# A GpSimd memset moved behind the first v load, with an early idle matmul waiting on it

## The chip, the cores and the metric

The kernel runs on one core of one Trainium2 chip. The metric is the device time of one execution in microseconds (us). The six executions of the kernel before that were timed beside the change lie from 288.93 to 289.5 us (0.2%). Ratios compare the mean time of one kernel's fast runs with the mean of the other's fast runs of the same rounds, on the same chip, so a ratio is not quite the ratio of the medians that stand beside it.

## The reference

Chunked attention (8 batches, 8 heads, 576 positions in chunks of 64, head size 64), followed by a two-layer network with a swish whose slope is learned:

```python
scores = scale * q_c @ k_c.T          # per chunk of 64
attn = softmax(scores)
x = (attn @ v_c)                      # rearranged to (4608, 512)
h = x @ w_in                          # (4608, 2048)
g = h * sigmoid(beta * h)
out = g @ w_out                       # (4608, 512), float32
```

## The kernel before

The network's matmuls fill the span: those of its two layers (L322 and L354 on the page) are busy for 136.7 and 131.3 us of 287.5. What matters here is the start, where the first attention blocks are made while the array's clock is still slow: the idle matmuls start mostly 0.427 us apart up to 7.23 us and 0.216 us apart from 9.00 us on (the trace's record of the clock has it fast from 7.69). TensorE's stream begins with 78 tiny matmuls and 14 idle ones on zeros, put there for the clock's sake, of which the fourth (16 columns wide) reads `late`, so that it waits on a memset by GpSimd. `emit_T_half(0)` uses the raw first half of q and k, cast by ScalarE; `emit_T_half(1)` uses the second half ("the q half", "the k half" below), loaded and cast by GpSimd's own transfers.

```python
nc.vector.memset(tiny, 0.0)
nc.vector.memset(idle, 0.0)
nc.vector.memset(braw, 0.0)
nc.vector.memset(vbig[:, :, :, D:D + 1], 1.0)
for a, eng, dst in ((0, nc.sync, raw0), (1, nc.gpsimd, qk0[1])):
    for i, src in enumerate((q, k)):
        eng.dma_start(out=dst[i], in_=...)      # the second pair: q half, k half
...                                             # beta, by the sync queue
nc.gpsimd.memset(late, 0.0)
for i in range(4):
    load_v(i)
...                                             # identity, weights, further loads
emit_tiny(78)
warm = idle_bank()
emit_idle(3, 512, warm)
nc.tensor.matmul(out=warm[:, 0:16], lhsT=idle[:, 0:128], rhs=late)
emit_idle(10, 512, warm)
emit_T_half(0)                                  # VectorE transposes q and k, first half
emit_sc_half(0, 0)                              # first scores
emit_ex_half(0, 0)
emit_idle(6, 512, idle_bank())                  # (shortened)
emit_T_half(1)                                  # second half: needs q half and k half
nc.vector.transpose(out=bt, in_=braw)
emit_sc_half(0, 1)                              # second scores
emit_ex_half(0, 1)
emit_sc_half(1, 0)
emit_idle(2, 512, warm)
emit_pv(0, ("s", "p"))                          # needs v loads 0 and 1
...
```

The softmax here doesn't subtract the row's maximum and nothing guards it: scores larger than these inputs give would overflow.

## Time and profile before

| | kernel before |
|---|---|
| time, median of 3 (range) | 288.98 us (288.93 to 289.1) |
| span in the profile | 287.5 us |
| TensorE busy | 281.2 us, 98% |
| k half, from issue to landing | 2.12 to 9.74 us |
| second scores start | 10.91 us |

The prediction shows the lines of the page, the chain and the timeline. A chain is read from the bottom up: each piece was released by the one above it. A timeline line gives start, length, engine, source line, operation and count; a bracket at its end gives the idle time of the engine just before and what ended it.

### The profile page before, as it was taken

The page shows a single profiled execution, that of the slowest core. Times are in us where ns is not written, and L with a number is a line of the kernel's source. Part 1 is how long each engine was busy: PE and PEld are TensorE (multiplying, and loading weights), DVE is VectorE, ACT ScalarE, POOL GpSimd, SP SyncE. Part 2 cuts the span into 40 slices and gives each one's busy share as a digit, 9 for nine tenths or more (in the row PEclk, how much of TensorE's full clock was granted, in tenths as well). Part 3 has the DMA queues.
Part 4 walks back from the last instruction along what each step waited for, and adds up shares of the span by engine and source line. Part 5 has one row for each costly group of instructions (what it writes and reads, how often), then busy time and mean ns, then how long its engine had stood idle before and what let it go on. Part 6 is the DMA issues. An engine that isn't in the chain of part 4 may idle for free.

```text
span 287.5 us, 6650 instructions
## 1 busy us (share of the span) xinstructions
PE 281.2 (98%) x2779; PEld 136.2 (47%) x2779; DVE 141.4 (49%) x253; ACT 146.7 (51%) x224; POOL 95.7 (33%) x125
## 2 busy tenths in 40 slices
PE   8889999999999999999999999999999999999995
PEld 4464456545544444444444444444444444444444
DVE  2678444776567554534454445444453536333300
ACT  4377218774557545454545454555445544444411
POOL 8743579397172992060907060000000000000000
PEclk9999999999999999999999999999999999999999
DMA  8999999999999999999999999614252212010012
GB/s 197 174 197 206 169 178 209 211 163 173 153 94 182 155 176 179 153 130 159 132 167 134 145 155 142 134 49 110 75 113 73 73 39 73 36 39 36 36 73 75
DMA packets 139997, 37.14 MB, mean 129 GB/s; under 512 B 126912, under 2 KB 135488, under 8 KB 139968
## 3 DMA queue, kind: packets, MB, share of 16 engines
q0 software_dynamic: 99136, 17.83, 79.7%
q1 hardware_dynamic: 40688, 18.83, 30.5%
q8 instruction: 22, 0.36, 0.5%
q14 instruction: 7, 0.06, 0.1%
q10 hardware_dynamic: 144, 0.07, 0.1%
HBM read 36.71 MB, written 9.44 MB: 161 GB/s over the span
## 4 chain that ended last, share of the span: by engine, by line
PE 94%; DMA 3%; ACT 1%; issue 1%; DVE 0%; POOL 0%; DVEq 0%; POOLq 0%
PE hps L322 44%; PE ops L354 42%; DMA h<-in_k_dram 3%; PE x L264 2%; PE sc L236 1%; PE sc L223 1%; PE ops L580 1%; ACT xt L297 1%; PE xp L296 1%; PE sc L196 0%; ACT et L206 0%; POOL h L394 0%; PE warm L374 0%; PE xp L304 0%; DVE xt L297 0%
## 5 line engine op out<-in xcount | busy, mean ns | idle before, releaser
L336 DVE SCALAR_TENSOR_TENSOR gt<-sg,hps 128x512 f16<-128x512 f32 (+1 forms) x153 | 99.1, 654 | 108.5 <-ACT sg L332 108.3
L332 ACT ACTIVATE sg<-hps,beta 128x512 f32<-128x512 f32 (+1 forms) x153 | 100.4, 663 | 74.0 <-PE hps L322 73.9
L322 PE MATMUL hps<-xt,win 128*128 128x512 f16 (+1 forms) x612 | 136.7, 367 | 0.8 <-ACT xt L297 0.7
L354 PE MATMUL ops<-wout,gt 128*128 128x512 f16 x560 | 131.3, 379 | 0.0
L322 PEld LDWEIGHTS <-win 128*128 128x128 f16 x612 | 58.0, 98 | 61.9 <-issue 1.0
L354 PEld LDWEIGHTS <-gt 128*128 128x128 f16 x560 | 53.7, 98 | 63.1
L364 ACT ACTIVATE osb<-ops 128x512 f32<-128x512 f32 x35 | 20.9, 598 | 42.2 <-PE ops L354 42.2
L112 POOL DMA_DIRECT2D vbig<-in_v_dram x40 | 34.0, 872 | 10.3 <-DMA wout<-in_moe_w_out_dram 3.7
L98 POOL DMA_DIRECT2D qu<-in_q_dram x22 | 18.7, 865 | 39.5 <-DMA qT<-qu 37.2
L280 DVE TENSOR_TENSOR x<-x,rd 128x512 f16<-128x512 f32 x34 | 23.5, 692 | 1.3
L98 POOL DMA_DIRECT2D ku<-in_k_dram x22 | 18.9, 880 | 0.1
L278 DVE RECIPROCAL rd<-x 128x8 f32<-128x8 f32 x34 | 6.8, 201 | 11.1 <-PE x L264 11.1
L245 ACT ACTIVATE et<-sc 128x1024 f16<-128x1024 f32 (+1 forms) x8 | 6.4, 811 | 8.2 <-PE sc L236 8.2
L229 ACT ACTIVATE et<-sc 128x1024 f16<-128x1024 f32 x10 | 10.1, 1015 | 0.0
L264 PEld LDWEIGHTS <-et 64*64 64x64 f16 x576 | 6.0, 107 | 7.3 <-issue 3.4
L374 PE MATMUL warm<-idle 128*128 128x512 f16 x24 | 8.6, 515 | 0.0
L264 PE MATMUL x<-vbig,et 64*64 64x65 f16 x544 | 7.8, 195 | 0.2 <-ACT et L206 0.2
L104 POOL DMA_DIRECT2D ku<-in_k_dram x9 | 6.8, 755 | 2.5 <-DMA win<-in_moe_w_in_dram 1.3
L104 POOL DMA_DIRECT2D qu<-in_q_dram x9 | 6.8, 767 | 1.9 <-DMA win<-in_moe_w_in_dram 1.1
L592 DVE TENSOR_SCALAR osb<-ops 128x256 f32<-128x256 f32 (+1 forms) x2 | 0.7, 358 | 12.1 <-PE ops L580 12.1
L130 POOL DMA_DIRECT2D win<-in_moe_w_in_dram x8 | 6.0, 751 | 1.2 <-DMA h<-in_k_dram 0.8
L177 DVE STREAM_TRANSPOSE t<-h 128x512 f32<-128x512 f32 x4 | 4.2, 1084 | 4.2 <-ACT h L176 3.7
(46 smaller groups left out, 69.3 us busy)
## 6 DMA issues: line engine op xcount, KB each, us to landing
out_dram<-osb SPq DMA_DIRECT2D x35, 256.0 KB, 3.4
vbig<-in_v_dram POOLq DMA_DIRECT2D x32, 128.0 KB, 7.6
qu<-in_q_dram POOLq DMA_DIRECT2D x20, 128.0 KB, 5.3
ku<-in_k_dram POOLq DMA_DIRECT2D x20, 128.0 KB, 6.6
win<-in_moe_w_in_dram POOLq DMA_DIRECT2D x8, 256.0 KB, 9.7
wout<-in_moe_w_out_dram POOLq DMA_DIRECT2D x4, 512.0 KB, 12.4
qu<-in_q_dram POOLq DMA_DIRECT2D x3, 256.0 KB, 7.3
ku<-in_k_dram POOLq DMA_DIRECT2D x3, 256.0 KB, 8.9
```

Of the source, the lines that this page charges most:

```text
L98: nc.gpsimd.dma_start(out=tv[off:off + n, sp], in_=src[b, :, s:s + n, :].rearrange("h p d -> p h d"),)
L104: nc.gpsimd.dma_start(out=t[off // 2:(off + n) // 2], in_=src[b, :, s:s + n, :].rearrange("h (p r) d -> p h r d", r=2),)
L112: nc.gpsimd.dma_start(out=vbig[off:off + n, i, :, 0:D], in_=v[b, :, s:s + n, :].rearrange("h p d -> p h d"),)
L229: nc.scalar.activation(out=et, in_=sc, func=ACTF.Exp, scale=scale)
L264: nc.tensor.matmul(out=(x[0][64 * c:64 * c + 64, r, g, 0:D + 1] if len(x) == 1 else x[r][64 * c:64 * c + 64, g, 0:D + 1]), lhsT=(et[64 * r ...
L280: nc.vector.tensor_tensor(out=o, in0=z[..., 0:D], in1=rd[:, r].to_broadcast(list(o.shape)), op=ALU.mult)
L322: nc.tensor.matmul(out=hps[:, 0:n], lhsT=w_in16[m // 2][:, kk, (m % 2) * 128:(m % 2) * 128 + 128], rhs=xr[:, c0 // CH:(c0 + n) // CH, 2 * ...
L332: nc.scalar.activation(out=sg[:, 0:n], in_=hps[:, 0:n], func=ACTF.Tanh, scale=beta2[:, m:m + 1])
L336: nc.vector.scalar_tensor_tensor(out=gt_t[j][:, m, c0:c0 + n], in0=sg[:, 0:n], scalar=1.0, in1=hps[:, 0:n], op0=ALU.add, op1=ALU.mult,)
L354: nc.tensor.matmul(out=ops, lhsT=gt_t[j][:, kk, t * 128:(t + 1) * 128], rhs=w_out16[kk // 4][:, kk % 4, :], start=(kk == 0), stop=(kk == K ...
L364: nc.scalar.activation(out=osb, in_=ops, func=ACTF.Copy, scale=0.5)
L374: nc.tensor.matmul(out=d[:, 0:w], lhsT=idle[:, 0:128], rhs=idle[:, 0:w])
```

## The change

The intent is to move the idle matmuls a little later by letting the matmul on `late` wait longer: the memset is issued behind the first v load instead of ahead of it.

```diff
-        nc.gpsimd.memset(late, 0.0)
         for i in range(4):
             load_v(i)
+            if i == 0:
+                nc.gpsimd.memset(late, 0.0)
```

## The prediction

> **What bounds the kernel now.** I read the page's busy shares first, then the chain of work that ended last, then the timeline of the first 18 us, and last the individual idle matmuls. From the page:
>
> ```profile
> span 287.5 us, 6650 instructions
> PE 281.2 (98%) x2779; PEld 136.2 (47%) x2779; DVE 141.4 (49%) x253; ACT 146.7 (51%) x224; POOL 95.7 (33%) x125
> PE hps L322 44%; PE ops L354 42%; DMA h<-in_k_dram 3%; PE x L264 2%; PE sc L236 1%; PE sc L223 1%; PE ops L580 1%; ACT xt L297 1%; PE xp L296 1%; PE sc L196 0%; ACT et L206 0%; POOL h L394 0%; PE warm L374 0%; PE xp L304 0%; DVE xt L297 0%
> ```
>
> The second line says that TensorE is busy nearly throughout; the third, that the chain is TensorE for 94% of the span, with one transfer of a k tile in it (3%). From 18.0 us on, the stage windows give 262.85 us busy of 263.00. Nothing in the change reaches that part except by the time at which it starts and the clock at which it starts. So the question is what the change does to the first 18 us. The chain over these 20 us, in order of time, begins:
>
> ```profile
> 1.24 0.88 POOL h L394
> 2.12 7.62 DMA h<-in_k_dram
> ...
> 9.77 0.06 DVE t L177
> ...
> 10.71 0.18 DVE bt L425
> ...
> 10.91 0.71 PE sc L196 x58
> ```
>
> Its columns are start, length and what. The path is: GpSimd issues the half of k that it casts on the way (from 2.12 us), this takes 7.62 us to land, VectorE transposes it from 9.77 us and then the beta tile from 10.71, and only at 10.91 does TensorE come onto the path. The idle matmuls before it are on no path[...]. The memset and its matmul lie here:
>
> ```profile
> 2.12 0.76 POOL L394 DMA_DIRECT2D h<-in_k_dram  x1
> 2.86 0.15 POOL L401 MEMSET late<- 128x16 f16 x1
> 2.90 3.54 POOL L112 DMA_DIRECT2D vbig<-in_v_dram  x4
> 2.12 1.46 PE L374 MATMUL warm<-idle 128*128 128x512 f16 x3
> 3.37 0.22 PE L417 MATMUL warm<-late,idle 128*128 128x16 f16 x1
> 3.44 4.41 PE L374 MATMUL warm<-idle 128*128 128x512 f16 x10
> 8.40 0.45 PE L196 MATMUL sc<-t,t 32*64 32x64 f16 x32 [0.55 <-DVE t L177]
> 8.78 1.47 PE L374 MATMUL warm<-idle 128*128 128x512 f16 x6
> 10.91 0.71 PE L196 MATMUL sc<-t,t 32*64 32x64 f16 x64 [0.66 <-DVE bt L425]
> ```
>
> (First the GpSimd timeline, then TensorE's: start, length, engine, line, what; the bracket is idle time ahead of it and its releaser.) The memset ends at 2.86 + 0.15 = 3.01 us. Its matmul starts at 3.37 with no bracket: it waits for nothing, since the three idle matmuls ahead occupy the array till then. **The wait is empty today**, by 0.36 us. Then the array is idle twice before the path reaches it: 0.55 us before 8.40 and 0.66 us before 10.91, both times for VectorE.
>
> [...] in the records of single instructions the idle matmuls start 0.427 us apart up to the last of the ten, at 7.231, and those after the first scores 0.216 us apart (9.000, 9.216, 9.432). So the fast clock came somewhere from 7.66 (7.231 + 0.427) to 8.40 or soon after. The column of granted clock reads 1.0 throughout; it doesn't show this. [...] four v loads take 3.54 us of GpSimd, 0.885 us each, one after another, and a memset behind one has to wait for it.
>
> **The change part by part.** No instruction is removed or added; one memset moves behind one v issue.
>
> *GpSimd.* The first v issue moves from 2.90 to about 2.86, 0.04 us earlier. It takes 0.885 us of its turn, so the memset runs at 2.86 + 0.885 = 3.74 and ends at 3.89. In the kernel before it overlapped its neighbours so far that it cost only 2.90 - 2.86 = 0.04 us, so the other three v loads start when they do now (3.78 for the second), and so does everything behind them. The k half on the path is issued at 2.12, ahead of all of this. Sum on the transfers: 0.00 on the path, 0.04 us earlier for one v load that is used at 12.08 and lands after about 7.6 us, near 10.5.
>
> *TensorE.* A finished memset released the first tiny matmul 0.05 us later (0.82 + 0.09 = 0.91, start at 0.96). So the matmul on `late` starts at 3.89 + 0.05 = 3.94 instead of 3.37: the wait becomes real, about 0.57 us of idle array. From this matmul to the last of the ten idle ones is 7.231 - 3.364 = 3.867 us, so the last starts at 3.94 + 3.87 = 7.81, and its 0.427 us of streaming end at 8.24. The scores can't start before 8.40, when VectorE releases them. **The 0.57 us come out of the idle stretch before 8.40** (7.66 to 8.40 is 0.74 us of real slack by start-to-start spacing), and 0.16 us of it are left. Sum on the scores: 0.00.
>
> *After that.* Even if the scores slipped by 0.1 or 0.2 us, the six idle matmuls end near 10.08 (9.863 + 0.216) and TensorE then waits until 10.91. That is 0.8 us of further cushion, and ScalarE's first exponential at 8.91 is followed by idle time until 11.41. So the direct sum on the path is 0.0 us.
>
> *Clock.* The new hole lies at 3.37 to 3.94. [...]
>
> **The rivals.**
>
> [...] Cost: six idle matmuls at 0.427 for 0.216 add 6 x 0.211 = 1.27 us, of which 0.8 us is cushion, so 0.45 us; the second scores and the two idle matmuls behind them at half speed (0.6 + 0.43 us now) add perhaps another 0.5 us: about +1 us, 290.0. Against it: three timed runs before lie within 0.17 us of each other[...]; and the new dense stretch runs from 3.94 almost without a hole to 10.1, longer than the old one from 2.11 to 7.66. In the extreme, [...] the 6 us or so of TensorE work from 10.9 to 18.0 (6.16 us busy) would nearly double: +6 us, 295. I hold this for very unlikely.
>
> *The hole makes the clock come earlier or the start better.* A reason to put a wait there would be to push idle work closer to the first scores[...]. But the clock is fast at 8.78 already, and no idle matmul before 10.91 is on the path, so there is nothing to win in this phase: 288.9 at best, unless timed executions of the kernel before often started cold beyond 10.9, which their narrow spread speaks against.
>
> *GpSimd is delayed.* If the memset between two software-made transfers costs its 0.15 us in full, or more for a change of task, all later issues shift by 0.1 to 0.3 us. The weights are needed at 15.62 and the ones on the path were issued before; k doesn't move. Cost 0 to 0.1 us, 289.1.
>
> **Range and chances.** Direct sum 0.0 us, so the middle is the time before, 289.0. The spread of executions (0.17 us here; the profiled run took 289.26) gives about 0.3 us either way; the later clock, at maybe one in seven, stretches the upper side by 1 us; hence 288.6 to 289.8. Two per cent is 5.8 us, more than anything in the first 18 us could give back, and only the extreme clock case reaches it upwards: faster 0.01, slower 0.02.
>
> **What would show it right or wrong.** In the changed profile: memset at about 3.74; matmul on `late` near 3.94, with idle time ahead of it put down to GpSimd; ten idle matmuls 0.427 us apart, the last at about 7.8; first scores still at 8.40 with the idle time ahead nearly gone; six idle matmuls behind them 0.216 us apart; k half landing near 9.75, second scores at 10.91, steady part from 18.0. Wrong if: the six idle matmuls are 0.427 apart (later clock); the first scores start when the idle matmuls let them, above 8.5; the k half lands at another time by over 0.2 us; or the memset finishes long after 3.9.

The prediction's sum came to 0.0 us (0.00 on the transfers, 0.00 on the scores), so to 289.0 us. Its range of 288.6 to 289.8 adds 0.3 us either way for the spread of executions and 1 us on the upper side for a later clock. The transfers called "software-made" are those of queue 0, which the page lists as `software_dynamic` (99136 packets).

## More of the kernel before

The view of the DMA queues, taken for 7.1 to 7.3 us of the kernel before, lists beside the data queues (columns: queue, kind, packets, megabytes, share of the time of the 16 engines):

```profile
q8 instruction: 1, 0.02, 29.2%
```

This is a packet of instructions: 16 KB, begun at 7.17 us and 0.93 us long by its record in the trace. The whole execution has 22 of them. From the first to the last, TensorE starts 5389 instructions (185 and 5574 started), which makes 257 between one and the next on average; singly it is 94 to 434. I take these packets to feed TensorE's instruction stream and call the first of them the fetch.

## The result

The changed kernel takes 289.55 us (median of 6, 289.34 to 289.81) against 289.13 (288.93 to 289.5) before: ratio 1.0014, 95% interval 1.0001 to 1.0027. By the 2% rule that is the same time; it is inside the predicted range, but 0.4 us above the kernel before, where the prediction's sum was 0.0.

The page of the changed kernel has the same shape:

```profile
span 287.7 us, 6650 instructions
PE 280.8 (98%) x2779; PEld 136.1 (47%) x2779; DVE 141.3 (49%) x253; ACT 146.7 (51%) x224; POOL 95.6 (33%) x125
```

The timeline of the start shows what was expected of GpSimd and TensorE:

```profile
2.86 0.91 POOL L112 DMA_DIRECT2D vbig<-in_v_dram  x1
3.73 0.16 POOL L404 MEMSET late<- 128x16 f16 x1
3.94 0.17 PE L418 MATMUL warm<-late,idle 128*128 128x16 f16 x1 [0.36 <-POOL late L404]
3.97 3.77 PE L374 MATMUL warm<-idle 128*128 128x512 f16 x10
8.42 0.45 PE L196 MATMUL sc<-t,t 32*64 32x64 f16 x32 [0.69 <-DVE t L177]
8.80 1.47 PE L374 MATMUL warm<-idle 128*128 128x512 f16 x6
11.21 0.71 PE L196 MATMUL sc<-t,t 32*64 32x64 f16 x64 [0.94 <-DVE bt L426]
```

The memset runs at 3.73 and its matmul at 3.94, so the hole is there. The first scores hardly move (8.42 for 8.40), and the six idle matmuls take 1.47 us as before, so the clock was fast in time. Yet the second scores start at 11.21 instead of 10.91. The chain says why:

```profile
2.13 7.93 DMA h<-in_k_dram
...
10.07 0.06 DVE t L177
...
11.01 0.18 DVE bt L426
...
11.21 0.71 PE sc L196 x62
```

The k half lands 0.31 us later (7.93 us for 7.62 from issue), and everything behind it is later by 0.30. I compared the start of every hundredth matmul of the two traces: from the 200th to the last, the changed kernel is 0.30 to 0.31 us behind at each one. So in these two profiles the loss is made before 11.2 us and carried to the end.

Why should a transfer issued at the same 2.12 us land later? The DMA view of the changed kernel for 7.9 to 8.1 us has the instruction packet that stood at 7.17 before:

```profile
q8 instruction: 1, 0.02, 30.4%
```

By its record it runs from 7.93 to 8.90 us. The landings tell the rest. The trace has 16 reports of the k half's landing, each of which I take for one share of the transfer (no record says what a report stands for): in the changed kernel 15 came by 8.68 us, and the last alone at 10.05. Before, 14 came by 8.67, one at 9.44 and the last at 9.74. In the changed kernel one share of the transfer is late by itself. And it stays behind: of each of the four v loads that follow, too, the last report comes 1.05 to 1.13 us after the fifteenth. The instruction packet of 16 KB took 0.97 us here, where one of 512 bytes in GpSimd's queue takes 0.06 us. If it holds up one share of the transfer, and not the others, it would do this. The packet records don't name a DMA engine, so this was a theory to be tested:

- **Theory A.** The wait on `late` holds up TensorE's instruction fetch. The later memset moves the fetch later by 0.76 us, onto the tail of the k half, which lands later.
- **Theory B.** The first v load, now issued 0.04 us earlier, takes DMA time from the k half.
- **Theory C.** The landing varies by itself, and the 0.4 us are noise.
- **The hole.** The idle time in the array itself costs, by way of the clock or otherwise.

### The profile page after: what moved, and what is told of

It is laid out like the page before. It is cut to its first block, busy times and chain, and to the rows that moved or that the text cites. A ratio compares the mean times of both kernels' runs of the same rounds, so it can differ in the third digit from the quotient of the medians.

```text
span 287.7 us, 6650 instructions
## 1 busy us (share of the span) xinstructions
PE 280.8 (98%) x2779; PEld 136.1 (47%) x2779; DVE 141.3 (49%) x253; ACT 146.7 (51%) x224; POOL 95.6 (33%) x125
## 3 DMA queue, kind: packets, MB, share of 16 engines
q0 software_dynamic: 99136, 17.83, 79.8%
HBM read 36.71 MB, written 9.44 MB: 160 GB/s over the span
## 4 chain that ended last, share of the span: by engine, by line
PE 93%; DMA 3%; ACT 1%; issue 1%; DVE 0%; POOL 0%; DVEq 0%; POOLq 0%
PE hps L322 44%; PE ops L354 42%; DMA h<-in_k_dram 3%; PE x L264 2%; PE sc L236 1%; PE sc L223 1%; PE ops L581 1%; ACT xt L297 1%; PE xp L296 1%; PE sc L196 0%; ACT et L206 0%; POOL h L394 0%; PE warm L374 0%; PE xp L304 0%; DVE xt L297 0%
## 5 line engine op out<-in xcount | busy, mean ns | idle before, releaser
L112 POOL DMA_DIRECT2D vbig<-in_v_dram x40 | 34.3, 881 | 10.1 <-DMA wout<-in_moe_w_out_dram 3.7
L229 ACT ACTIVATE et<-sc 128x1024 f16<-128x1024 f32 x10 | 10.1, 1015 | 0.0
```

The lines of the kernel that those rows point to most:

```text
L112: nc.gpsimd.dma_start(out=vbig[off:off + n, i, :, 0:D], in_=v[b, :, s:s + n, :].rearrange("h p d -> p h d"),)
L229: nc.scalar.activation(out=et, in_=sc, func=ACTF.Exp, scale=scale)
```

## The experiments

Times of the fetch, of the 16th report of the k half and of the memset are from the records in each run's trace; the second scores from its timeline. All runs gave correct results. Times from records can differ by 0.01 us from those of the views.

| run | memset ends | fetch starts | k half landed | second scores | median us | ratio to before (95%) |
|---|---|---|---|---|---|---|
| before | 3.00 | 7.17 | 9.74 | 10.91 | 289.13 | |
| change | 3.89 | 7.93 | 10.05 | 11.21 | 289.55 | 1.0014 (1.0001 to 1.0027) |
| aa_before | 3.00 | 7.18 | 9.75 | 10.91 | 289.09 | 0.9998 (0.9986 to 1.0010) |
| after_again | 3.89 | 7.99 | 10.06 | 11.23 | 289.55 | 1.0017 (1.0004 to 1.0030) |
| gap_only | 3.94 | 7.94 | 10.05 | 11.21 | 289.63 | 1.0013 (1.0001 to 1.0025) |
| v_early_only | 1.19 | 5.44 | 9.57 | 10.74 | 289.25 | 1.0013 (0.9997 to 1.0029) |
| tiny68 | 3.01 | 12.74 | 9.06 | 11.52 | 294.80 | 1.0190 (1.0159 to 1.0220) |
| after_tiny68 | 3.89 | 12.86 | 8.97 | 10.56 | 295.53 | 1.0199 (1.0166 to 1.0233) |
| late_after_v1 | 4.76 | 8.72 | 9.35 | 11.50 | 289.30 | 1.0000 (0.9982 to 1.0019) |
| tiny88 | 3.01 | 5.32 | 9.54 | 10.71 | 289.10 | 0.9994 (0.9979 to 1.0010) |
| after_tiny88 | 3.89 | 5.50 | 9.77 | 10.93 | 289.24 | 1.0002 (0.9985 to 1.0019) |
| late6_v1 | 4.77 | 8.91 | 8.71 | 10.18 | 288.63 | 0.9976 (0.9962 to 0.9991) |
| late8_v2 | 5.64 | 10.19 | 9.18 | 10.55 | 289.58 | 1.0015 (0.9996 to 1.0035) |
| late6_v0 | 3.89 | 7.80 | 9.88 | 11.05 | 289.48 | 1.0026 (1.0005 to 1.0047) |

### The two kernels again: aa_before, after_again

No edit.

> The kernel before, unchanged, timed against itself. All theories: ratio 1.000. It shows how far a ratio of the size measured for the change (1.0014) can come from noise alone: if this one departs from 1 by 0.001 or more, the 0.4 us of the change are not shown to be its own. In its profile the k half should land near 9.74 us, as in the first profile; if it lands anywhere from 9.4 to 10.1, the landing varies by itself.

> The changed kernel once more. Theory A (TensorE's later progress moves its instruction fetch, [...] from 7.17 to 7.93 us, onto the tail of the k half, which then lands at 10.05 instead of 9.74): fetch again near 7.9, k half near 10.05, ratio 1.001 to 1.002. Theory B (the first v load, issued 0.04 us earlier, takes DMA time from the k half): the same landing, with no tie to the fetch. Theory C (noise): ratio within 0.0005 of 1, the k half anywhere from 9.4 to 10.1.

Both held to theory A. The kernel before against itself gives 0.9998, with fetch and landing within 0.01 us of the first profile; the changed kernel again gives 1.0017, with fetch at 7.99 and landing at 10.06. Theory C falls: the landing does not vary by itself from 9.4 to 10.1; in the two profiles of each kernel it agrees within 0.01 us. The cost of the change is small but its own. One thing was not the same in after_again: a share of the raw k half landed at 6.92 us (6.18 in the first profile), so that VectorE released the first scores only at 9.15. The second scores started at 11.23 all the same, behind the k half.

The clock, by contrast, does vary. In the timeline of the kernel before, run again, the ten idle matmuls took 3.00 us instead of 4.41:

```profile
3.45 3.00 PE L374 MATMUL warm<-idle 128*128 128x512 f16 x10
8.37 0.45 PE L196 MATMUL sc<-t,t 32*64 32x64 f16 x32 [1.92 <-DVE t L177]
```

The trace's record of the clock has it fast from 4.86 us here and from 7.69 in the first profile of the same kernel, and the second scores start at 10.91 in both. So the moment of the fast clock does differ between executions, by 2.83 us in these two. In these two it cost nothing.

### One part of the change at a time: gap_only, v_early_only

```diff
# gap_only                                 # v_early_only
 nc.gpsimd.memset(late, 0.0)               -nc.gpsimd.memset(late, 0.0)
 for i in range(4):                        +nc.vector.memset(late, 0.0)   # ahead of braw's
     load_v(i)
+    if i == 0:
+        nc.gpsimd.memset(late, 0.0)
```

> The memset is done twice, at its old place and behind the first v issue; the matmul waits for the second. So the hole in TensorE is as in the changed kernel, but the first v load is issued at 2.90 us as in the kernel before. Theory A: as the changed kernel: matmul on late at 3.94, fetch near 7.9, k half near 10.05, +0.3 to +0.4 us, ratio 1.001 to 1.0015. Theory B: as the kernel before: k half near 9.74, ratio 1.000. Theory C: ratio 1.000, landing anywhere.

> The memset is done by VectorE at the start, so there is no hole in TensorE, and the first v load is issued at 2.86 us as in the changed kernel. Theory A: as the kernel before: matmul on late at 3.37, fetch near 7.2, k half near 9.74, ratio 1.000. Theory B: as the changed kernel: k half near 10.05, ratio 1.001 to 1.0015. Theory C: ratio 1.000, landing anywhere.

gap_only, with the first v load at its old 2.90 us, costs what the change costs: k half at 10.05, 0.5 us in the medians. v_early_only, with that load at 2.86 and no later wait, has the k half at 9.57, not at 10.05. Theory B falls by both landings. The ratio of v_early_only, 1.0013, is the one that theory B foretold, but two of its six times make it (290.07 and 290.70); the other four lie from 289.11 to 289.32.

For theory A the second run was a miss that taught something. It should have been like the kernel before, with the fetch at 7.2; the fetch came at 5.44. Its timeline has the matmul on `late` where it always was, with no idle time ahead of it:

```profile
2.12 1.46 PE L374 MATMUL warm<-idle 128*128 128x512 f16 x3
3.37 0.22 PE L417 MATMUL warm<-late,idle 128*128 128x16 f16 x1
```

The array did the same things at the same times as in the kernel before, up to the ten idle matmuls. Only the memset ended at 1.19 instead of 3.00. So a wait that costs the array nothing still goes with a later fetch (7.17 us with it, 5.44 without). My guess is that it holds the part of TensorE that issues instructions, and that this part reaches the wait before the array does; no record here shows this part. The expectations below call it the sequencer, and what they say of it is theory, as is a fetch that holds up one DMA engine. In eight runs in which, by theory A, the place that sets off the fetch lies behind the wait (before, change, aa_before, after_again, gap_only, late_after_v1, late6_v1, late6_v0), the fetch starts 3.9 to 4.2 us after the memset's end; in a ninth, late8_v2, it is 4.55 us.

The start of v_early_only is 0.17 us ahead of the kernel before, but its six times are 289.11 to 290.70 with a median of 289.25. The profiled one, 290.07, lost more than it had gained at 126.87 us, in its list of waits:

```profile
PE hps L322 <- DMA out_dram<-osb: 0.6, 1, 0.6
```

This is one wait that the kernel before has not. What made that transfer late is open; a further 0.22 us went between the 1700th and the 1800th matmul.

### Moving the fetch by moving the stream: tiny68, after_tiny68, tiny88, after_tiny88

If the fetch belongs to a place in the stream, ten tiny matmuls fewer put that place behind the first scores, and ten more put it ahead of the wait on `late`. The fetch did move so: to 12.74 us with 68 and to 5.32 with 88, from 7.17 with 78.

```diff
-emit_tiny(78)
+emit_tiny(68)    # tiny68; the same edit of the changed kernel is after_tiny68
+emit_tiny(88)    # tiny88, after_tiny88
```

> The kernel before with ten tiny matmuls fewer (68 for 78), so every later instruction of TensorE stands 20 places (10 weight loads, 10 matmuls) earlier in its stream. Theory A in the form the first runs gave it (a block of TensorE's instructions is fetched some 4.05 us after its sequencer passes a certain place just behind the wait on late): that place now lies behind the first scores, which wait until 8.4 us, so the fetch comes at about 12.4, after the k half. The k half then lands near 8.7 in place of 9.74, VectorE takes it when it is done with the q half at 9.3, and the second scores start near 10.45 in place of 10.91: about 0.45 us off, 288.7, ratio 0.9985. Rival (the landing depends on the hole in TensorE or on the order of GpSimd's issues alone): k half at 9.74, ratio 1.000.

> The changed kernel with 68 tiny matmuls. Theory A: the hole of 0.57 us is still there, but the fetch no longer hits the k half, so the cost of the change vanishes: k half near 8.7, second scores near 10.45, ratio 0.9985, the same as the 68 tiny matmuls alone within 0.1 us. Rival (the hole costs by itself): 0.3 to 0.4 us slower than the 68 tiny matmuls alone.

> The kernel before with ten tiny matmuls more (88). Theory A: the place of the fetch now lies ahead of the wait on late, so the fetch comes as early as in the run with the memset on VectorE, near 5.4 us or somewhat before, and the k half lands near 9.6, second scores near 10.75, about 0.15 us faster, ratio 0.9995, unless the fetch now holds up one of the raw loads (landing at 4.65 and 6.16), which would push the first scores and VectorE up to 0.9 us. Rival: k half at 9.74, ratio 1.000.

> The changed kernel with 88 tiny matmuls. In the kernel before with 88 the fetch came at 5.32 us, because its place in the stream then lies ahead of the wait on late. Theory A: the hole is still there (the matmul on late at 3.94 for 3.48), but the fetch no longer depends on the wait: fetch near 5.3, k half near 9.55, second scores near 10.7, 289.0 us, the same as 88 without the change (289.1) within 0.15 us and 0.45 us under the changed kernel. Rival (the hole costs by itself): 0.3 to 0.4 us over the 88 without the change: k half near 10.05, 289.5.

The two runs with 68 hit the fetch (12.74 and 12.86) and the k half (9.06 and 8.97, the lowest so far), and missed the time by 6 us. The timeline of tiny68 shows why:

```profile
13.26 0.24 PE L196 MATMUL sc<-t,t 32*64 32x64 f16 x5
15.20 0.41 PE L196 MATMUL sc<-t,t 32*64 32x64 f16 x27 [1.70 <-issue]
```

In the midst of a group of 32 matmuls TensorE stops for 1.70 us, and the profile finds nothing that it waits for. It stops behind the fifth of them; in after_tiny68 it stops behind the same fifth, for 2.83 us. That is after the same instruction, the 449th that TensorE starts, though 1.15 us earlier, and both go on at 15.2 us, some 2.4 us after their fetch began. From this I conclude that **TensorE had run out of instructions** (an inference: no record shows its store of them). Here a fetch that came after the k half's data was too late for the stream. The clock fell as well. The table of stages of tiny68 (columns: stage, its length, busy time and count of TensorE, its weight loads, VectorE, ScalarE and GpSimd, then the granted clock, DMA share and GB/s):

```profile
5.40:8.80 3.40, 1.56 (x38) 0.72 (x36) 2.57 (x3) 1.43 (x2) 3.33 (x7) 1.00 1.61 182
8.80:12.20 3.40, 3.40 (x83) 1.42 (x71) 1.48 (x3) 0.60 (x1) 3.01 (x5) 0.50 2.24 163
12.20:15.60 3.40, 1.70 (x86) 1.04 (x78) 1.93 (x6) 0.60 (x1) 1.69 (x3) 1.00 1.45 197
15.60:19.00 3.40, 2.96 (x45) 1.77 (x44) 0.92 (x4) 2.04 (x4) 1.92 (x4) 0.50 1.45 196
```

After a stage of 3.4 us with TensorE busy for half of it or less (1.56 and 1.70 us), the next stage is at half clock. This is no rule: in aa_before, TensorE was busy for 1.59 us of the 3.41 from 4.86 us on, and the clock stayed fast. How much of the 6 us is starvation and how much is clock these two runs don't separate, and because of them the time of after_tiny68 could not decide on the hole.

The runs with 88 went the other way. In tiny88 the fetch came at 5.32 and the k half at 9.54, as expected, and the six times lie from 289.04 to 289.15. With the change on top, the hole is there (the matmul on `late` at 3.94), and the fetch stays at 5.50 instead of following the memset. The k half lands at 9.77, not the 9.55 expected; 0.23 us of difference is left between the two profiles, beside 0.31 at 78, and 0.14 us in the medians, which come from two different sets of rounds. So the part of theory A that the fetch no longer follows the wait held, but that the cost goes with it is not shown by this pair. In this execution six reports of the k half came late, from 8.91 to 9.77, and not one alone, so something else held it up too. A rival is left by this pair: the memset's new place on GpSimd, or the hole, could delay the landing by itself. The pair with 68 answers it. There the fetch came after the k half both times, and the change did not make the k half land later (8.97 with it, 9.06 without).

### The wait moved in steps: late_after_v1, late8_v2, late6_v1, late6_v0

```diff
# late_after_v1: memset behind the second v load
-    if i == 0:
+    if i == 1:
# late6_v1: the same, and the matmul on late behind six idle matmuls
-emit_idle(3, 512, warm)
+emit_idle(6, 512, warm)
 nc.tensor.matmul(out=warm[:, 0:16], lhsT=idle[:, 0:128], rhs=late)
-emit_idle(10, 512, warm)
+emit_idle(7, 512, warm)
# late8_v2: memset behind the third v load, eight idle matmuls ahead, five behind
# late6_v0: the six and seven, memset behind the first v load as in the change
```

> The changed kernel with the memset behind the second v issue instead of the first: it ends near 4.8 us. Theory A: fetch 4.05 us later, near 8.85, when the k half's packets are all but through; k half near 8.8, second scores between 10.45 and 10.9 (the ten idle matmuls end up to 9.1 us and may hold the first scores), 0 to 0.45 us faster than the kernel before, ratio 0.9985 to 1.000. Rival (a longer hole costs more, in proportion): 0.6 to 0.8 us slower, ratio 1.0025.

late_after_v1 put the fetch at 8.72 as foreseen, and the k half landed at 9.35, earlier than in either kernel, which goes against any rule that a later wait means a later landing. But now the idle matmuls reached up to 9.27 us, the first scores started behind them at 9.20, and in the profiled execution the second scores at 11.50. So here the hole in the array did cost: it was longer than the slack ahead of the first scores (9.20 us for 8.40 in the kernel before). Its times spread from 288.70 to 289.82, ratio 1.0000.

> The changed kernel, memset behind the first v issue (ends 3.89), but the matmul on it stands after six idle matmuls instead of three, so the array reaches it at about 4.65 and there is no hole[...]. Theory A (the fetch follows the sequencer's wait): fetch near 7.95, k half near 10.05, second scores near 11.2, 289.5, ratio 1.001 to 1.0015, so the whole cost of the change without its hole. Rival (the hole in the array is what costs): no hole, no cost: k half near 9.75, 289.15, ratio 1.000.

late6_v0 is the sharpest test. The memset ends at 3.89 as in the change, but the array reaches the matmul on it only at 4.64 and loses nothing:

```profile
4.64 0.22 PE L418 MATMUL warm<-late,idle 128*128 128x16 f16 x1
4.72 2.59 PE L374 MATMUL warm<-idle 128*128 128x512 f16 x7
8.36 0.45 PE L196 MATMUL sc<-t,t 32*64 32x64 f16 x32 [1.05 <-DVE t L177]
...
11.05 0.71 PE L196 MATMUL sc<-t,t 32*64 32x64 f16 x64 [0.84 <-DVE bt L426]
```

There is no hole, and the cost is there: 289.48 for 289.11 in the medians of its rounds (the ratio of means, 1.0026, has one run of 291.43 in it). The k half lands at 9.88, a bit ahead of the 10.05 expected, because the fetch came at 7.80 and not at 7.95. With the fetch this late, the landing follows its end: in the four runs with the fetch on the tail of the k half (change, after_again, gap_only, late6_v0), the last report comes 1.15, 1.12, 1.13 and 1.14 us after the fetch packet ended (8.90, 8.94, 8.92, 8.75). In the two profiles of the kernel before it is 1.64 and 1.61 us, so this distance is not general. The rival of the hole falls for the change.

> The memset behind the second v issue (ends near 4.76), and the matmul on it after six idle matmuls instead of three, seven behind it. The wait is then nearly empty for the array (it would start at 4.65 anyway, so a hole of some 0.15 us)[...]. Theory A: fetch some 4.0 us later, near 8.75; k half from 9.0 to 9.35, second scores from 10.45 to 10.55, first scores at 8.4 to 8.5; about 0.4 us faster than the kernel before, 288.75, ratio 0.9985. If the fetch's place is ahead of the shifted wait, it comes near 5.4 and the gain is 0.2. Rival (the landing does not follow the wait of the sequencer): k half near 9.75, ratio 1.000.

late6_v1 puts the fetch at 8.91, behind the k half. All 16 reports of it are in by 8.71 us, the last no longer apart from the others (the one before it is at 8.63). The array has almost no hole:

```profile
4.82 0.17 PE L418 MATMUL warm<-late,idle 128*128 128x16 f16 x1
4.85 3.07 PE L374 MATMUL warm<-idle 128*128 128x512 f16 x7
8.34 0.45 PE L196 MATMUL sc<-t,t 32*64 32x64 f16 x32 [0.42 <-DVE t L177]
8.71 1.47 PE L374 MATMUL warm<-idle 128*128 128x512 f16 x6
10.18 0.71 PE L196 MATMUL sc<-t,t 32*64 32x64 f16 x64
```

The second scores start at 10.18, with no bracket: they come straight behind the six idle matmuls, and VectorE is done before them. The gain was underrated (10.45 to 10.55 expected). **This version beats both kernels**: 288.63 us, all six runs from 288.56 to 288.76, under every run of the kernel before in its rounds (288.93 and up). The medians are 0.56 us apart; the ratio of means, 0.9976 (0.9962 to 0.9991), also has two runs of the kernel before at 290.54 and 291.01 in it. By the 2% rule it is still the same time.

> The memset behind the third v issue (ends near 5.65), the matmul on it after eight idle matmuls, five behind it. Theory A: fetch near 9.6, wholly behind the k half, which lands near 9.0; VectorE's transposes end the earlier q half at 9.3, so second scores near 10.45; the fetch may hold up the first two v loads on one engine by up to 0.95 us (10.55 and 11.4 now, wanted from 11.6): 0.2 to 0.45 us faster than the kernel before, 288.7 to 288.95. If the fetch's place is ahead of the wait, it comes near 5.4 and the gain is 0.2.

late8_v2 moved the fetch further, to 10.19, and lost: the k half was in by 9.18, but now the second v load lands 8.49 us after its issue at 3.73 (the first four took 7.6 to 7.7 in the kernel before), which I put down to the packet. The timeline names this load, between the two halves of the first product with v:

```profile
12.27 0.60 PE L264 MATMUL y<-vbig,et 64*64 64x65 f16 x16 [0.22 <-DMA vbig<-in_v_dram]
```

The expectation had named this danger and given it too little weight.

## Why the prediction was right or wrong

The time and the chances were right: 289.55 lies within 288.6 to 289.8, and the class is "same". The direct sum of 0.0 us was wrong by 0.3 us in the profile, 0.4 in the medians. That the range still held it was luck: the 0.3 us that it allowed for noise end at 289.3, and the rest of its upper side was there for a later clock, which is not what came.

- **GpSimd's part** held: first v load at 2.86, memset at 3.73 to 3.89, second v load at 3.78.
- **TensorE's part** held for the array: matmul on `late` at 3.94, first scores at 8.42 (9.15 in after_again, for VectorE). The idle time ahead of them was 0.69 us and not nearly gone, because in that execution the clock was fast from 6.93 and the last idle matmuls went quicker (3.77 us for all ten, 4.41 in the kernel before).
- **The clock's part** held in its outcome: the six idle matmuls stayed at 0.216 us. One run of the changed kernel, after_again, had the fast clock only from 8.11 us, so the rival of a later clock can't be ruled out for other executions, but here it did not reach the path: the second scores started at 11.23, as the landing of the k half has it.
- **The step that failed** is "Sum on the transfers: 0.00 on the path", with its reason that the k half "is issued at 2.12, ahead of all of this". Behind it stands the sentence "**The wait is empty today**". It was empty for the array alone. v_early_only shows that the fetch of TensorE's instructions went with it even then: fetch 5.44 without it, 7.17 with it, the array alike up to that wait. Making it longer moved the fetch from 7.17 to 7.93 and the k half's last share from 9.74 to 10.05. The prediction had set as a sign of error that the k half lands over 0.2 us off; it landed 0.31 off.
- **None of the three rivals** was this one. The "delayed GpSimd" rival came nearest, at 0.1 us, but on the wrong transfers.

What is inferred and not seen: that fetch packet and late share are on the same DMA engine, as the records carry no engine's number. The steady distance from the end of the packet to the landing in four runs speaks for it, and so does the late share moving to the first v load in late6_v1 (15 reports by 9.45, the last at 11.02) and to the second in late8_v2 (15 by 10.89, the last at 12.22). Not every late report is the fetch's: in tiny68, after_tiny68, late_after_v1 and late8_v2, whose packet ended after the k half had landed, one to three reports still came 0.3 to 0.7 us behind the rest.

Open is also why the same packet delays more when it comes later. If a packet of 0.95 us held a share up once, I would expect the share to be late by as much wherever the packet falls. But the last report came 0.94 us behind the one before it with the fetch at 5.44 (v_early_only), 1.10 with it at 7.18 (aa_before), 1.24 at 7.80 (late6_v0) and 1.37 at 7.93 (change). So the runs tie the cost of the change to the moved fetch; why it is 0.31 us they don't show. Open, too: which place in the stream sets off the fetch, and what takes the 4 us from the wait to the packet.

## What to carry to other kernels

At the start of a kernel, look in the DMA queues for instruction packets (here 16 KB each; the first took 0.93 us before and 0.97 after the change), and see which data transfer they meet and how near TensorE is to running dry (here it stopped for 1.70 us in tiny68 and 2.83 in after_tiny68). In this kernel a wait without idle time in front of the array still went with a later fetch (7.17 us with it, 5.44 without), and the fetch moved when the wait was lengthened (to 7.93) and when the count of warm-up matmuls changed (5.32 with 88, 12.74 with 68); the k half's landing shifted each time (10.05, 9.54 and 9.06 us for 9.74). So look for the like after such an edit. When one of 16 reports of a transfer is late alone, as here at 10.05 us with the other 15 in by 8.68, look for what held that one.
